# Splitting work moved between units of a gated two-branch Hedgehog linear-attention kernel, and three orders changed

## The chip, the cores and the metric

The kernel runs on one core of one Trainium2 chip. The time is the device time of one execution in microseconds (us), as the median of several runs; before the change it is 357.98 us (3 runs, 357.31 to 358.96). One of the five engines multiplies matrices (PE, with its weight loads shown apart as PEld); DVE, ACT and POOL work elementwise on tiles of 128 partitions; SP only issues DMAs. ACT issues some DMAs too. Each engine takes its instructions in the order in which the program gives them.

## The reference

```python
def _ref(x, wqkv, w_phi, wo):              # 16 heads of 28, x is 2048 x 448
    q, k, v = split((x @ wqkv))
    pq = einsum("bhsd,hdf->bhsf", q, w_phi)
    pk = einsum("bhsd,hdf->bhsf", k, w_phi)
    phi_q = concat([softmax(pq), softmax(-pq)])
    phi_k = concat([softmax(pk), softmax(-pk)])
    kv = einsum("bhsf,bhsd->bhfd", phi_k, v)
    z  = sum over s of phi_k
    o  = (phi_q @ kv) / (phi_q @ z + 1e-6)
    return o @ wo
g = sigmoid((x * gate_w).sum(-1))
out = g * _ref(x, A weights) + (1 - g) * _ref(x, B weights)
```

## The kernel before

The 2048 rows are 16 tiles of 128; two tiles make a unit, so each branch has 8 units, numbered here 0 to 7 for branch A and 8 to 15 for branch B. All matmuls on the inputs are done as three products of a high and a low part: `split_x` (L105) and `high_wv`/`low_wv`, `high_wo`/`low_wo` (L136, L139, L416, L420) make them. The high part is a copy on ACT (L108, L131), the low part a subtraction on POOL (L110, L112, L134) or DVE. `proj` (L172) makes one unit's queries, keys or values with 22 matmuls (11 for each tile, listed in `TERMS`, line L181) of 448 columns; x chunks 4 to 6 and the lower half of chunk 3 are low parts. The feature weights are folded into the key and query weights first: `fold` (L159) runs 32 small matmuls (L151) into two PSUM tiles, `fold_out` copies each on ACT (L156) and subtracts on DVE (L157).

A unit's keys go through `k_shift` (DVE L195 to L197, POOL L198), `k_exp` (two exponentials on ACT, L202), `k_sums` (two sums and a reciprocal on DVE, L211 and L212, then two normalising products on POOL, L220) and `kv_acc` (64 short matmuls on PE, L245), which adds the unit to the state. Queries go through `q_front` (L272, L274, and stores of `uq` to `qd` in DRAM, L281) and `q_load` (L289, `tq` back from DRAM), `q_exp0`, `q_min`, `q_exp1` (ACT L297, DVE L301, POOL L305, ACT L312) and `q_turn` (a DVE transposition into `wtb`, L315). `num` (L327) multiplies them with the state; `a_turn` (L524), `n_rec`, `n_den`, `weights` (L339 to L360) and `n_mul` (L365) turn, normalise and gate the numerators, `n_add` (L369) adds the halves. `wtb` (two buffers) also holds raw key and query weights, raw x and, from unit 2 on, the output weights that `load_wo` brings and `low_wo` sends back to DRAM (`wod`, L423 and L424) in two parts: part c lies in buffer (c // 2) % 2.

The order is that of the text. It is written in three stages: a prologue (L373 to L405) with unit 0's values; a loop over branch A's units (L431 to L502); a loop over branch B's units (L532 to L581), which also does branch A's numerators; and a last stage in which `STEPS` lists steps by hand, with the output products (L773), the copy of a finished tile `oc` (L783) and its store `sw` (L787). In branch A's loop two tables say in which unit the splits are made: `WVS` for branch B's value weights, `WOS` for the output weights. SP's queue takes loads and stores in program order, so a store that waits for data holds back all behind it. The PSUM work tiles called `two` are three, taken in turn.

Of the kernel before, what the change touches and what calls it, by code (L numbers as in the profile page):

```python
# [10 lines left out]
AF = mybir.ActivationFunctionType  # L11
# [3 lines left out]
P = 128  # L15
S, D, H, DH = 2048, 448, 16, 28
NT = S // P
# [32 lines left out]
def hedgehog_mix(ctx: ExitStack, tc: tile.TileContext, xd, wv, wkt, wqt, wphi, wo, cmask, cpmask, out):  # L50


    nc = tc.nc
# [40 lines left out]
    wvs = [wp_.tile([P, 2, 4, DG], F32R, name="wva"), wp_.tile([P, 2, 4, D], F32R, name="wvb")]  # L94
    wq = [wp_.tile([P, 2, 4, D], F32R, name="wqa"), None]
# [9 lines left out]
    def split_x(g, lo, hi, *parts):  # L105
        r, t, h = [a[:, :, lo * P:hi * P] for a in (xraw[g], xg[g], xg[g].bitcast(F32))]
        if 0 in parts:
            nc.scalar.activation(t[:, 0:4], r, AF.Copy)  # L108
        if 1 in parts:
            nc.gpsimd.tensor_tensor(t[64:P, 3], r[64:P, 3], h[64:P, 3], OP.subtract)  # L110
        if 2 in parts:
            nc.gpsimd.tensor_tensor(t[:, 4:7], r[:, 0:3], h[:, 0:3], OP.subtract)  # L112
# [31 lines left out]
    def two_tile(i=None):  # L144
        if i is None:
            i = turn[0] = (turn[0] + 1) % 3
        return twos[i].tile([P, 2, 512], F32, name=f"two{i}")
# [11 lines left out]
    def fold(b, wt, dst):  # L159
        for c in range(0, 4, 2):  # L160
            ps = two_tile()
            for g in range(4):
                fold_mm(b, wt, ps, g, c)
            fold_out(ps, dst, c)
# [7 lines left out]
    def proj(u, w, ps, order=None):  # L172
        n = w.shape[3]
        for i, j in order or [(i, j) for i in range(2) for j in range(11)]:
            if i is None:
                warm(j)
                continue
            t = 2 * u + i
            x, o = xg[t // 4], (t % 4) * P
            xc, k, wc = TERMS[j]  # L180
            nc.tensor.matmul(ps[:, i, :n], x[:, xc, o:o + P], w[:, k, wc], start=j == 0, stop=j == 10)  # L181
        return ps
# [7 lines left out]
    def k_shift(k, ps):  # L190
        p4 = hb(ps[:, :, :D])
        mx = ph.tile([P, 2, 2, H], F32, name="mx")
        e = es[k] = ph.tile([P, 2, HA * DH], F32, name="e")
        e5 = e.rearrange("p s (w h f) -> p s w h f", w=2, f=DH)
        nc.vector.tensor_reduce(mx[:, 0], p4, AX.X, OP.max)  # L195
        nc.vector.tensor_tensor(e5[:, 0], p4, mx[:, 0, :, :, None].to_broadcast([P, 2, H, DH]), OP.subtract)
        nc.vector.tensor_reduce(mx[:, 1], e5[:, 0], AX.X, OP.min)  # L197
        nc.gpsimd.tensor_tensor(e5[:, 1], mx[:, 1, :, :, None].to_broadcast([P, 2, H, DH]), e5[:, 0], OP.subtract)  # L198
# [23 lines left out]
    def k_sums(k):  # L222
        k_sums0(k)
        k_sums1(k)

    def v_out(k, ps):
        v = vs[k % 2]
        nc.scalar.activation(v[:, :, :, :, :DH].rearrange("p w j q f -> p w (j q) f"), hb(ps[:, :, :D]), AF.Copy)  # L228
        if k < NU:
            nc.scalar.activation(glog[:, 2 * k:2 * k + 2], ps[:, :, D], AF.Copy)  # L230
# [131 lines left out]
    def n_mul(k, lo=0, hi=8):  # L362
        c3 = cview(k).rearrange("p r s a m -> p (r s) a m")[:, :, lo:hi, :DH]
        dd = sms[k][1].rearrange("p r s a -> p (r s) a")[:, :, lo:hi, None]
        nc.gpsimd.tensor_tensor(c3, c3, dd.to_broadcast([P, 8, hi - lo, DH]), OP.mult)  # L365
# [22 lines left out]
    def warm(n):  # L388
        for i in range(n):
            nc.tensor.transpose(pw[:, 0, :P], ident, ident)  # L390
# [7 lines left out]
    for q in range(4):  # L398
        nc.vector.tensor_scalar(bd[:, :, :, q * DH:(q + 1) * DH], wp[:, :, :, :DH], mask[:, q:q + 1], None, op0=OP.mult)
    pv = proj(0, wvs[0], two_tile(), TERMS0)  # L400
    split_x(0, 2, 4, 0, 1, 2)
    v_out(0, pv)
    fold(0, wt, wk[0])
    split_x(1, 0, 4, 0, 1, 2)
    v_out(1, proj(1, wvs[0], two_tile()))  # L405


    def wo_part(c):
# [3 lines left out]
    def load_wo(*cs):  # L412
        for c in cs:
            nc.sync.dma_start(wo_part(c)[0], wos[:, HP * c:HP * (c + 1), :])
# [9 lines left out]
        nc.sync.dma_start(wod[1][:, c], st[0])  # L424


    WVS = {1: (0, 1, 2), 3: (3,)}
    WOS = {3: (0, 1), 5: (2, 3), 6: (4, 5), 7: (6,)}
    FRONTS = {2: 0, 5: 1}
    pq = None  # L430
    for u in range(NU):  # L431

        if u in (2, 4):
            split_x(u // 2 + 1, 0, 4, 0)
        for c in WVS.get(u, ()):
            high_wv(1, c)
        if u == 5:
            nc.gpsimd.memset(eq[:, :, :, :, DH:], 0.0)
            for b in range(2):
                nc.gpsimd.memset(kvs[b], 0.0)  # L440
        if pq is not None:
            q_front(FRONTS[u - 1], pq)
            q_load(FRONTS[u - 1])
            pq = None
        pk = proj(u, wk[0], two_tile())
        if u > 1:
            k_sums(u - 1)
        if u in (2, 4):
            split_x(u // 2 + 1, 0, 4, 1)
        k_shift(u, pk)  # L450
        if u == 1:
            k_sums(0)
        if u == 2:
            pq = proj(0, wq[0], two_tile())
            kv_acc(0)
        if u > 1:
            pv = proj(u, wvs[0], two_tile())
            v_out(u, pv)
        k_exp(u)

        if u == 0:
            wtqa = load_wt(wtb[0], wqt[0])
            load_x(2, 0, 4)
            for c in range(0, 4, 2):
                load_wv(1, c)
        if u == 1:
            wtkb = load_wt(wtb[1], wkt[1])
            nc.sync.dma_start(wos.rearrange("g (a f) n -> g a (f n)", f=DH),
                              wo.rearrange("(a g f) n -> g a (f n)", g=4, f=DH))
        if u in (2, 4):  # L470
            split_x(u // 2 + 1, 0, 4, 2)
        for c in WVS.get(u, ()):
            low_wv(1, c, nc.gpsimd)
        for c in WOS.get(u, ()):
            high_wo(c)
            low_wo(c)
        if u == 2:
            load_wo(0, 1)
            load_x(3, 0, 4)
        if u == 4:  # L480
            load_wo(2, 3)
        if u == 5:
            load_wo(4, 5)
            start.close()
            mid = ctx.enter_context(tc.tile_pool(name="mid", bufs=1, side="right"))
            wtqb = load_wt(mid.tile([P, 2048], F32, name="ctr"), wqt[1])
        if u == 6:
            load_wo(6)
        if u > 1:
            kv_acc(u - 1)  # L490
        if u == 1:
            fold(0, wtqa, wq[0])
        if u == 3:
            fold(1, wtkb, wk[1])
        if u == 5:
            pq = proj(FRONTS[u], wq[0], two_tile())
        if u == 6:
            q_exp0(0)
            q_min(0)
            q_exp1(0)  # L500
        if u == 7:
            q_turn(0)  # L502
# [29 lines left out]
    for u in range(NU):  # L532
        k = NU + u
        f, m, n = u + 2, u + 1, u - 1
        if u == 2:
            ctr[1] = mid.tile([P, 2048], F32, name="ctr")
        pq = proj(f % NU, wq[f // NU], two_tile())
        if n >= 0:
            a_turn(n)
            n_rec(n)  # L540
        q_exp0(m)
        q_min(m)
        q_exp1(m)
        if n >= 0:
            n_den(n)
            weights(n, nc.gpsimd)
            n_mul(n)
        else:
            k_sums(k - 1)
        q_front(f, pq)  # L550
        q_load(f)
        pk = proj(u, wk[1], two_tile())
        if u == 0:
            kv_acc(k - 1)
            state_copy(0)
        else:
            k_sums(k - 1)
        k_shift(k, pk)
        if u == 0:
            state_turn(0)  # L560
            q_turn(m)
            fold(1, wtqb, wq[1])
        pv = proj(u, wvs[1], two_tile())
        v_out(k, pv)
        k_exp(k)
        if u > 0:
            q_turn(m)
        if u == NU - 1:
            woh, wol = [wp_.tile([P, 7, D], F32R, name=n) for n in ("wkb", "wvb")]
            for w, d in ((woh, wod[0]), (wol, wod[1])):  # L570
                nc.sync.dma_start(w.bitcast(F32), d)
        if n >= 0:
            a_add(n)
        if u == 4:
            nc.gpsimd.tensor_scalar(gate[:, 1], gate[:, 0], -1.0, 1.0, op0=OP.mult, op1=OP.add)
        ts = nums[u] = [two_tile(), two_tile()]
        num(u, [t[:, i] for t in ts for i in range(2)])
        if u == 0:
            gates()
        else:  # L580
            kv_acc(k - 1)  # L581
# [4 lines left out]
    obs = [ob[:, i] for i in range(2)]  # L586
# [4 lines left out]
    nps, turns, outs = [], [None, None], [None, None]  # L591
# [188 lines left out]
        products(t, ((1, woh),))  # L780

    def oc(t):
        nc.scalar.activation(obs[t % 2], outs[t % 2][:, :D], AF.Copy)  # L783
        hls.pop(t)

    def sw(t):
        nc.sync.dma_start(out[t * P:(t + 1) * P, :], obs[t % 2])  # L787

    acts = dict(q=q, qf=qf, mx=mx, cp=cp, qs=qs, sq=sq, aq=aq, sl=sl, e0=e0, mn=mn, ms=ms, e1=e1, qt=qt, at=at, na=na, sa=sa, da=da,
                wa=wa, ma=ma, aa=aa, sd=sd, ks=ks, km=km, kv=kv, sc=sc, st=st, ss=ss, num=num_, bt=bt, nr=nr, sm=sm, nd=nd, wt=wt_,  # L790
# [47 lines left out]
```

## Time and profile before

| | before |
|---|---|
| median of 3 runs | 357.98 us (357.31 to 358.96) |
| profiled execution, its own time | 359.09 us |
| its span, first to last instruction | 357.2 us |
| granted TensorE clock, mean | 0.998 |
| DVE, ACT, POOL busy | 270.1, 121.8, 261.5 us |
| one load or store of a part of the output weights | 224 KB |
| load of `ctr`; one of the four stores of a unit's queries | 896 KB; 112 KB |

The profiled execution is 1.1 us above the median of the runs; 1.9 us of its time lie outside its span. PE is busy nearly the whole span, so the time can be read from the places where PE's next group of matmuls starts late. In a timeline row stand the start, the duration, the engine, the line, the operation with output and input tile, the count, and in brackets how long the engine had been idle and who ended that.

### The profile page before, as it was taken

Reading aid. Unit: us, or ns where it says so; the run is one execution under the profiler, and the core shown is the slowest. Engines: PE = TensorE matmul, PEld = TensorE weight load, DVE = VectorE, ACT = ScalarE, POOL = GpSimd, SP = SyncE. Lnnn points to the kernel's source line nnn. Section 1 sums busy time; section 2 is a strip of 40 time slices with the busy share of each in tenths; the row PEclk is TensorE's granted clock in tenths of the full one; section 3 lists DMA queues with packets and bytes.
Section 4 is the critical chain, followed back from the end, with each engine's and each line's share of the span. In section 5 each row is a group of like instructions: output and inputs, shape, how many; then the busy total and the mean of one; then the engine's idle time right before and its main releaser. Section 6 shows DMA issues by size and latency. Waiting matters only on the chain.

```text
span 357.2 us, 8435 instructions
## 1 busy us (share of the span) xinstructions
PE 346.2 (97%) x3599; PEld 304.6 (85%) x3599; DVE 270.1 (76%) x312; ACT 121.8 (34%) x171; POOL 261.5 (73%) x226
## 2 busy tenths in 40 slices
PE   7999899999999999999999999999999999999995
PEld 6889789988987889798898989888888978888894
DVE  4118765643967749998989898899899999988840
ACT  4433532534054241315133131412224454434331
POOL 2453897497476606988889788886779999999850
PEclk9999999999999999999999999999999999999999
DMA  7795225300753402241313332249662461664111
GB/s 236 221 319 173 114 79 193 135 25 14 210 157 141 129 1 61 75 126 61 103 54 104 106 104 65 94 162 352 160 226 84 140 196 57 180 180 128 53 52 51
DMA packets 33733, 45.75 MB, mean 128 GB/s; under 512 B 11408, under 2 KB 27008, under 8 KB 33408
## 3 DMA queue, kind: packets, MB, share of 16 engines
q1 hardware_dynamic: 28688, 41.20, 36.9%
q10 hardware_dynamic: 5008, 4.02, 3.5%
q8 instruction: 28, 0.46, 0.5%
q14 instruction: 9, 0.07, 0.1%
HBM read 27.29 MB, written 19.53 MB: 131 GB/s over the span
## 4 chain that ended last, share of the span: by engine, by line
PE 65%; DMA 12%; POOL 8%; DVE 8%; issue 3%; ACT 2%; SPq 1%; ACTq 0%; POOLq 0%; DVEq 0%
PE two L181 39%; PE out L773 16%; PE two L327 4%; DMA qd<-uq 4%; POOL e L220 3%; PE kv L245 3%; DMA xrb<-in_xt 2%; POOL xg L112 1%; DMA wtb<-wos 1%; DVE sm L211 1%; DVE wtb L315 1%; ACT e L202 1%; DMA wp<-in_wphi 1%; DMA wod<-wtb 1%; PE two L151 1%
## 5 line engine op out<-in xcount | busy, mean ns | idle before, releaser
L181 PE MATMUL two<-wka,xg 128*128 128x448 f32 x352 | 73.8, 365 | 0.0
L181 PEld LDWEIGHTS two<-wka,xg 128*128 128x128 f32 x352 | 65.2, 188 | 5.6 <-issue 0.8
L220 POOL TENSOR_TENSOR e<-e,rs 128x896 f32<-128x896 f32 x32 | 53.9, 1706 | 19.1 <-DVE rs L212 19.1
L228 ACT ACTIVATE vs<-two 128x896 f32<-128x896 f32 x16 | 14.7, 920 | 97.6 <-PE two L181 97.6
L181 PE MATMUL two<-wva,xg 128*128 128x450 f32 x176 | 39.4, 373 | 1.9 <-ACT wva L131 1.0
L211 DVE TENSOR_REDUCE sm<-e 128x32 f32<-128x896 f32 x32 | 33.1, 1077 | 8.6 <-ACT e L202 8.6
L181 PE MATMUL two<-wqa,xg 128*128 128x448 f32 x176 | 38.0, 371 | 1.0 <-DVE wqa L157 1.0
L315 DVE STREAM_TRANSPOSE wtb<-xrb 128x2048 f32<-128x2048 f32 x16 | 36.6, 2290 | 2.3 <-ACT glog L230 2.3
L181 PEld LDWEIGHTS two<-wva,xg 128*128 128x128 f32 x176 | 32.8, 189 | 6.2 <-POOL xg L112 1.1
L181 PE MATMUL two<-wvb,xg 128*128 128x448 f32 x176 | 37.2, 366 | 0.0
L181 PE MATMUL two<-wkb,xg 128*128 128x448 f32 x176 | 36.5, 362 | 0.0
L181 PEld LDWEIGHTS two<-wqa,xg 128*128 128x128 f32 x176 | 32.4, 188 | 4.8 <-DVE wqa L157 1.4
L198 POOL TENSOR_TENSOR e<-mx,e 128x896 f32<-128x896 f32 x16 | 27.3, 1704 | 12.5 <-DVE mx L197 9.2
L181 PEld LDWEIGHTS two<-wvb,xg 128*128 128x128 f32 x176 | 33.0, 188 | 2.7
L181 PEld LDWEIGHTS two<-wkb,xg 128*128 128x128 f32 x176 | 33.0, 188 | 2.3
L773 PE MATMUL out<-wkb,e 128*128 128x448 f32 x154 | 34.7, 369 | 0.1
L202 ACT ACTIVATE e<-e 128x896 f32<-128x896 f32 x32 | 28.7, 945 | 17.7 <-POOL e L198 17.6
L773 PEld LDWEIGHTS out<-wkb,e 128*128 128x128 f32 x154 | 28.5, 188 | 4.1 <-issue 0.8
L305 POOL TENSOR_TENSOR xrb<-qmn,tq 128x896 f32<-128x896 f32 x16 | 28.1, 1758 | 2.7 <-issue 2.2
L272 DVE TENSOR_REDUCE qmx<-two 128x32 f32<-128x896 f32 x14 | 15.1, 1077 | 16.6 <-PE two L181 16.6
L365 POOL TENSOR_TENSOR wva<-wva,cdd 128x896 f32<-128x896 f32 (+1 forms) x12 | 26.5, 2211 | 0.9
L365 POOL TENSOR_TENSOR ctr<-ctr,cdd 128x896 f32<-128x896 f32 (+1 forms) x12 | 26.5, 2209 | 0.6
(105 smaller groups left out, 583.5 us busy)
## 6 DMA issues: line engine op xcount, KB each, us to landing
tq<-qd SPq DMA_DIRECT2D x16, 448.0 KB, 4.7
qd<-uq ACTq DMA_DIRECT2D x32, 112.0 KB, 2.7
qd<-uq SPq DMA_DIRECT2D x32, 112.0 KB, 2.1
od<-wva SPq DMA_DIRECT2D x8, 448.0 KB, 2.5
wqa<-od SPq DMA_DIRECT2D x8, 448.0 KB, 4.4
out<-bd SPq DMA_DIRECT2D x16, 224.0 KB, 3.6
wod<-wtb SPq DMA_DIRECT2D x14, 224.0 KB, 2.0
xrb<-in_xt SPq DMA_DIRECT2D x2, 1024.0 KB
```

What stands on the lines that cost most here:

```text
L181: nc.tensor.matmul(ps[:, i, :n], x[:, xc, o:o + P], w[:, k, wc], start=j == 0, stop=j == 10)
L198: nc.gpsimd.tensor_tensor(e5[:, 1], mx[:, 1, :, :, None].to_broadcast([P, 2, H, DH]), e5[:, 0], OP.subtract)
L202: nc.scalar.activation(es[k][:, s], es[k][:, s], AF.Exp)
L211: nc.vector.tensor_reduce(sm[:, s], e[:, s].rearrange("p (h f) -> p h f", f=DH), AX.X, OP.add)
L220: nc.gpsimd.tensor_tensor(e3, e3, rs[:, s, :, None].to_broadcast([P, HA, DH]), OP.mult)
L228: nc.scalar.activation(v[:, :, :, :, :DH].rearrange("p w j q f -> p w (j q) f"), hb(ps[:, :, :D]), AF.Copy)
L272: nc.vector.tensor_reduce(mx, p4, AX.X, OP.max)
L305: nc.gpsimd.tensor_tensor(eq[:, 1, :, :, :DH], mn.rearrange("p c a -> p a c")[:, :, :, None].to_broadcast([P, 8, 4, DH]), tview(k), OP.sub ...
L315: nc.vector.transpose(wtb[k % 2], eq.rearrange("p s a c f -> p (s a c f)"))
L327: nc.tensor.matmul(banks[r][32 * g:32 * g + 32, 256 * s:256 * s + 256], kvt[b][32 * r:32 * r + 32, s, g], eT[32 * r:32 * r + 32, s, g], st ...
L365: nc.gpsimd.tensor_tensor(c3, c3, dd.to_broadcast([P, 8, hi - lo, DH]), OP.mult)
L773: nc.tensor.matmul(outs[t % 2][:, :D], (hi, lo)[x][:, c], w[:, c], start=x == 0 and n == 0 and c == 0, stop=x == 1 and c == 6)
```

## The change

The last two tiles of the first four x tiles are split one by one, not as a pair. Unit 1's values are projected with the terms in another order: for each tile first the six products that need only high parts of x (0, 1, 2, 7, 8, 9), then chunk 3 (6), then the low parts (3, 4, 5), then chunk 3 with the low weights (10). The splits of branch B's value weights go from units 1 and 3 to units 2 and 3. Those of output weights 4 and 5 go from unit 6 to unit 5 and part 6 from unit 7 to unit 6, with their loads a unit earlier. The query fold goes ahead of unit 0's key sums and unit 1's exponentials. In branch B's second unit the normalising products of unit 8's keys go ahead of unit 0's numerators. The last tile is copied out half by ACT and half by DVE, and stored by two DMAs.

```diff
-    split_x(0, 2, 4, 0, 1, 2)
+    for i in range(2, 4):
+        split_x(0, i, i + 1, 0, 1, 2)
...
-    v_out(1, proj(1, wvs[0], two_tile()))
+    v_out(1, proj(1, wvs[0], two_tile(), [(i, j) for i in range(2) for j in (0, 1, 2, 7, 8, 9, 6, 3, 4, 5, 10)]))
...
-    WVS = {1: (0, 1, 2), 3: (3,)}
-    WOS = {3: (0, 1), 5: (2, 3), 6: (4, 5), 7: (6,)}
+    WVS = {2: (0, 1), 3: (2, 3)}
+    WOS = {3: (0, 1), 5: (2, 3, 4, 5), 6: (6,)}
...
         if u == 1:
+            fold(0, wtqa, wq[0])
             k_sums(0)
...
         if u == 4:
-            load_wo(2, 3)
+            load_wo(2, 3, 4, 5)
         if u == 5:
-            load_wo(4, 5)
+            load_wo(6)
...
-        if u == 6:
-            load_wo(6)
         if u > 1:
             kv_acc(u - 1)
-        if u == 1:
-            fold(0, wtqa, wq[0])
...
             weights(n, nc.gpsimd)
-            n_mul(n)
+            if u > 1:
+                n_mul(n)
...
             k_sums(k - 1)
+            if u == 1:
+                n_mul(n)
...
     def oc(t):
-        nc.scalar.activation(obs[t % 2], outs[t % 2][:, :D], AF.Copy)
+        n = D if t < NT - 1 else D // 2
+        nc.scalar.activation(obs[t % 2][:, :n], outs[t % 2][:, :n], AF.Copy)
+        if n < D:
+            nc.vector.tensor_copy(obs[t % 2][:, n:], outs[t % 2][:, n:D])
...
     def sw(t):
-        nc.sync.dma_start(out[t * P:(t + 1) * P, :], obs[t % 2])
+        n = D if t < NT - 1 else D // 2
+        if n < D:
+            nc.scalar.dma_start(out[t * P:(t + 1) * P, :n], obs[t % 2][:, :n])
+        nc.sync.dma_start(out[t * P:(t + 1) * P, D - n:], obs[t % 2][:, D - n:])
```

On PE no group of matmuls changes its place. On DVE, in unit 1 of branch A, before (`wqa` is the folded query weight, `sm` and `rs` the sums and reciprocals of units 0 and 1, `two` the PSUM tile):

```order
L197 TENSOR_REDUCE mx<-e 128x32
L211 TENSOR_REDUCE sm<-e 128x32 x2
L212 RECIPROCAL rs<-sm 128x64
L157 TENSOR_TENSOR wqa<-two_378,wqa 128x896
L157 TENSOR_TENSOR wqa<-two_389,wqa 128x896
L211 TENSOR_REDUCE sm<-e 128x32 x2
L212 RECIPROCAL rs<-sm 128x64
```

And in the changed kernel, the same place on DVE:

```order
L197 TENSOR_REDUCE mx<-e 128x32
L157 TENSOR_TENSOR wqa<-two_364,wqa 128x896
L157 TENSOR_TENSOR wqa<-two_375,wqa 128x896
L211 TENSOR_REDUCE sm<-e 128x32 x2
L212 RECIPROCAL rs<-sm 128x64
L211 TENSOR_REDUCE sm<-e 128x32 x2
L212 RECIPROCAL rs<-sm 128x64
```

The two subtractions of the fold now stand ahead of unit 0's sums; on ACT the fold's two copies (L156) likewise stand ahead of unit 1's two exponentials, and the three copies of value weights that stood between are gone from there.

On SP, around units 4 to 6 of branch A, before (`wtb` holds output weights, `wos` is their rearranged copy in DRAM, `ctr` takes branch B's raw query weights, `qd` and `tq` are unit 1's queries on their way through DRAM):

```order
L414 DMA wtb_122<-wos 128x1x448 x2
L423 DMA wod_85<-wtb_122 128x448
L424 DMA wod_86<-wtb_122 128x448
L423 DMA wod_85<-wtb_122 128x448
L424 DMA wod_86<-wtb_122 128x448
L414 DMA wtb_121<-wos 128x1x448 x2
L117 DMA ctr<-in_wqt 112x4x512
L281 DMA qd_89<-uq_128 32x4x224 x2
L289 DMA tq_130<-qd_89 128x896
L423 DMA wod_85<-wtb_121 128x448
L424 DMA wod_86<-wtb_121 128x448
```

In the changed kernel, from the last of the loads of parts 4 and 5 on:

```order
L415 DMA wtb_121<-wos 128x1x448 x2
L424 DMA wod_85<-wtb_122 128x448
L425 DMA wod_86<-wtb_122 128x448
L424 DMA wod_85<-wtb_122 128x448
L425 DMA wod_86<-wtb_122 128x448
L424 DMA wod_85<-wtb_121 128x448
L425 DMA wod_86<-wtb_121 128x448
L424 DMA wod_85<-wtb_121 128x448
L425 DMA wod_86<-wtb_121 128x448
L415 DMA wtb_122<-wos 128x1x448
L117 DMA ctr<-in_wqt 112x4x512
L281 DMA qd_89<-uq_128 32x4x224 x2
```

Four more stores now stand ahead of the load of `ctr` and of unit 1's queries, which stood ahead of them.

On POOL, at the second unit of branch B, before (`cdd` are the weights of unit 0's numerators in `wva`, `e` the keys' features):

```order
L360 TENSOR_TENSOR cdd<-crs,cden 128x64
L365 TENSOR_TENSOR wva<-wva,cdd 128x64x28
L220 TENSOR_TENSOR e<-e,rs 128x896 x2
L198 TENSOR_TENSOR e<-mx,e 128x896
L369 TENSOR_TENSOR wva<-wva 128x4x8x28
```

And in the changed kernel:

```order
L360 TENSOR_TENSOR cdd<-crs,cden 128x64
L220 TENSOR_TENSOR e<-e,rs 128x896 x2
L365 TENSOR_TENSOR wva<-wva,cdd 128x64x28
L198 TENSOR_TENSOR e<-mx,e 128x896
L369 TENSOR_TENSOR wva<-wva 128x4x8x28
```

The long product on the numerators (L365) changes places with the two products on unit 8's keys (L220); the next units' order is as before.

## The prediction

> **What bounds the kernel now.** I read the page's busy line first, then the timeline of PE, then for each late start of PE the timelines of the engines it waited for.
>
> ```profile
> PE 346.2 (97%) x3599; PEld 304.6 (85%) x3599; DVE 270.1 (76%) x312; ACT 121.8 (34%) x171; POOL 261.5 (73%) x226
> ```
>
> PE is busy 346.2 of 357.2 us and the change takes no matmul away: what can be won are PE's late starts and the two ends. In PE's timeline I compare the distance between starts of neighbouring groups, since the modelled ends of matmuls overlap the next start.
>
> ```profile
> 16.56 0.86 PE L181 MATMUL two<-wva,xg 128*128 128x450 f32 x3
> 18.20 4.18 PE L181 MATMUL two<-wva,xg 128*128 128x450 f32 x19 [0.77 <-POOL xg L112]
> 22.22 8.98 PE L181 MATMUL two<-wka,xg 128*128 128x448 f32 x44
> ...
> 34.52 4.66 PE L181 MATMUL two<-wka,xg 128*128 128x448 f32 x22
> 40.16 4.75 PE L181 MATMUL two<-wqa,xg 128*128 128x448 f32 x22 [0.98 <-DVE wqa L157]
> ...
> 60.52 0.99 PE L245 MATMUL kv<-e,vs 128*29 128x56 f32 x64
> ...
> 94.22 4.68 PE L181 MATMUL two<-wva,xg 128*128 128x450 f32 x22
> 98.83 0.99 PE L245 MATMUL kv<-e,vs 128*29 128x56 f32 x64
> 99.76 4.67 PE L181 MATMUL two<-wka,xg 128*128 128x448 f32 x22
> 104.27 4.66 PE L181 MATMUL two<-wva,xg 128*128 128x450 f32 x22
> 109.79 0.99 PE L245 MATMUL kv<-e,vs 128*29 128x56 f32 x64 [0.86 <-POOL e L220]
> ...
> 115.31 4.57 PE L181 MATMUL two<-wkb,xg 128*128 128x448 f32 x22
> 120.34 0.99 PE L245 MATMUL kv<-e,vs 128*29 128x56 f32 x64 [0.46 <-POOL e L220]
> ...
> 144.48 1.50 PE L327 MATMUL two<-wtb,kvt 32*32 32x256 f32 x64
> 146.82 0.99 PE L245 MATMUL kv<-e,vs 128*29 128x56 f32 x64 [0.84 <-POOL e L220]
> ...
> 162.73 0.99 PE L245 MATMUL kv<-e,vs 128*29 128x56 f32 x64
> ```
>
> Undisturbed, 22 value matmuls take 98.83 - 94.22 = 4.61 us to the next start, 22 key or query matmuls 104.27 - 99.76 = 4.51. Against these, five starts are late: unit 1's values by (22.22 - 16.56) - 4.61 = 1.05; the first queries by (40.16 - 34.52) - 4.51 = 1.13; the state of unit 6 by (109.79 - 104.27) - 4.61 = 0.91; that of unit 7 by (120.34 - 115.31) - 4.51 = 0.52; that of unit 8, by its bracket, 0.84. Together **4.45 us**. Each of the five is where one part of the change works. Times below are those of the run of before; a shift says by how much PE has come forward by then.
>
> **The x tiles and the order of terms (1.05).**
>
> ```profile
> 14.33 1.06 ACT L108 ACTIVATE xg<-xrb 128x1024 fp32r<-128x1024 f32 x1 [4.48 <-DMA xrb<-in_xt]
> ...
> 9.98 0.46 POOL L110 TENSOR_TENSOR xg<-xrb,xg 64x128 fp32r<-64x128 f32 x1 [2.86 <-ACT xg L108]
> 10.52 1.01 POOL L112 TENSOR_TENSOR xg<-xrb,xg 128x384 fp32r<-128x384 f32 x1
> ...
> 17.09 2.09 DVE L157 TENSOR_TENSOR wka<-two,wka 128x896 fp32r<-128x896 f32 x2 [7.26 <-ACT wka L156]
> ```
>
> The copy of two tiles starts at 14.33, when the data lands; PE stopped after three matmuls, for the low part. Cut in two, each copy costs at least 0.53 and at most 1.06, so the first is done by 15.4; its subtractions for one tile take 9.98 to 11.53 = 1.55, to about 17.0 at the latest, the second tile's to 18.55. PE starts unit 1 at 16.56 and now has six products of 0.21 (4.61 / 22) that need no low part, until 17.82, and one more that needs L110 alone. The second tile is begun 11 x 0.21 = 2.3 later, at 18.87, after all of it is there. The wait goes wholly, even by the upper ends: **1.05**. The extra copy pushes ACT's next work back by at most 1.06, and with it the folded key weight, from 19.18 to 20.24 at worst; the keys now start at 22.22 - 1.05 = 21.17, so it costs nothing, with 0.9 to spare.
>
> **The fold ahead of exponentials and sums (1.13).**
>
> ```profile
> 31.98 1.79 ACT L202 ACTIVATE e<-e 128x896 f32<-128x896 f32 x2 [8.58 <-POOL e L198]
> ...
> 38.09 1.70 ACT L156 ACTIVATE wqa<-two 128x896 fp32r<-128x896 f32 x2
> ...
> 33.48 1.09 DVE L197 TENSOR_REDUCE mx<-e 128x32 f32<-128x896 f32 x1
> 34.49 2.07 DVE L211 TENSOR_REDUCE sm<-e 128x32 f32<-128x896 f32 x2
> 36.59 0.55 DVE L212 RECIPROCAL rs<-sm 128x64 f32<-128x64 f32 x1
> 39.02 2.09 DVE L157 TENSOR_TENSOR wqa<-two,wqa 128x896 fp32r<-128x896 f32 x2 [1.87 <-ACT wqa L156]
> ```
>
> The fold's matmuls end just before 34.52; ACT came to its copies only at 38.09, behind three copies of value weights and unit 1's exponentials. Now they follow unit 0's exponentials (done 33.77), and the second waits for PE: done at about 35.5. DVE, free at 34.57, subtracts until about 36.8, 2.2 us before the queries can start at 34.52 + 4.51 = 39.03. All **1.13** are won; with 1.05 the shift is 2.18. What is late next: unit 0's sums and reciprocal follow the subtractions (2.07 + 0.55, to 39.4), POOL's products on its keys take 3.37 (row at 95.01 below), to 42.9, and PE wants them at 39.03 + 4.51 = 43.5. Margin 0.6; if the fold's products ran a microsecond longer, 0.4 would come back here.
>
> **The splits of weights.** The three copies and subtractions of value weights leave unit 1; two go to unit 2, one more to unit 3.
>
> ```profile
> 55.33 3.37 POOL L220 TENSOR_TENSOR e<-e,rs 128x896 f32<-128x896 f32 x2 [1.39 <-DVE rs L212]
> ...
> 95.01 3.37 POOL L220 TENSOR_TENSOR e<-e,rs 128x896 f32<-128x896 f32 x2 [4.48 <-DVE rs L212]
> ...
> 102.41 2.28 POOL L134 TENSOR_TENSOR wtb<-wtb 128x448 fp32r<-128x448 f32 x2 [2.37 <-ACT wtb L131]
> ...
> 106.36 3.38 POOL L220 TENSOR_TENSOR e<-e,rs 128x896 f32<-128x896 f32 x2
> ...
> 110.11 2.31 DVE L315 STREAM_TRANSPOSE wtb<-xrb 128x2048 f32<-128x2048 f32 x1 [2.30 <-ACT glog L230]
> ...
> 105.77 4.21 DMA wod<-wtb
> ```
>
> A subtraction is 2.28 / 2 = 1.14. In unit 2 two of them meet 1.39 of idle POOL, 0.9 too little: the products at 55.33 end 0.9 later, at 59.6, before PE's state at 60.52. Cost nothing; uncovered, 0.9. In unit 5 the two added subtractions (2.28) meet 4.48 of idle at 95.01: nothing. In unit 6 one of two goes, so the products at 106.36 begin 1.14 sooner, end at 108.6, and PE can start at 104.27 + 4.61 = 108.88: **0.91** won, with a margin of 0.28 only. In unit 7 the profile names ACT for DVE's wait of 2.30 at 110.11, but that ACT work was long done; the chain of waits has the store of output weights from `wtb` there, landing at 109.98. Parts 4 and 5 are now stored a unit earlier, so the transposition, and behind it unit 7's sums, come up to 2.3 sooner, and POOL's last subtraction of unit 7 is gone: **0.52** won.
>
> **Products ahead of the numerators (0.84).**
>
> ```profile
> 140.99 0.55 DVE L212 RECIPROCAL rs<-sm 128x64 f32<-128x64 f32 x1
> ...
> 140.21 3.22 POOL L365 TENSOR_TENSOR wva<-wva,cdd 128x1792 f32<-128x1792 f32 x1
> ...
> 153.57 3.22 POOL L365 TENSOR_TENSOR ctr<-ctr,cdd 128x1792 f32<-128x1792 f32 x1
> 157.53 3.37 POOL L220 TENSOR_TENSOR e<-e,rs 128x896 f32<-128x896 f32 x2 [0.74 <-DVE rs L212]
> ```
>
> The keys' products now wait for their reciprocal, 141.54, rather than for L365: 141.6 to 145.0, ahead of PE's 145.98. **0.84** won. In exchange everything from L365 on slides: POOL's work from 140.21 to 153.57 has no gap, 13.36 us, and now starts at 141.6, so the next L365 starts at 155.0 instead of 153.57 and unit 9's products at 155.0 + 3.2 = 158.2 instead of 157.53, to 161.6. PE wants them at 162.73 - 0.84 = 161.89. Margin 0.3; without the 0.74 of idle the loss would be 0.7. After that unit POOL is back in step.
>
> **The last tile.**
>
> ```profile
> 352.99 0.54 ACT L783 ACTIVATE bd<-out 128x448 f32<-128x448 f32 x1 [3.72 <-PE out L773]
> 353.56 0.81 SPq L787 DMA_DIRECT2D out<-bd  x2
> ```
>
> Two stores end the kernel: tile 15's, and behind it on SP tile 14's, whole. Half a copy on ACT beside half on DVE costs between half of 0.54 and all of it, so both stores start 0 to 0.27 sooner; the halves add a DMA on ACT's queue beside SP's issue of 0.4 each. Bounds -0.3 to +0.4 (one issue), I take **0.2** won. The Trainium skill, DMA: Bandwidth & Descriptors, Anatomy of one DMA, speaks against small transfers: about 2.0 us fixed and bytes over 436 GB/s; by it a half of 115 KB lands an estimated 0.26 us before a whole, which would make the sum 0.26 larger if the half came last. No run here shows its fixed part by itself, and tile 14's whole store comes last.
>
> **The rivals.**
>
> *New waits take a third.* Three margins are 0.6 or less (units 0, 6 and 9). If each was missed by half a microsecond, 3.15 of the 4.65 below remain: 354.8. For it: POOL's spans are rough. Against it: each duration stands in a row.
>
> *Nothing comes through.* The last stage has a list of steps of its own; if DVE and POOL, not PE, set its pace, the time won ahead of it is waited off there: about 357.5, from the tail alone. Against it: PE's share is 97% over all.
>
> *The stores hold up the queries: slower.*
>
> ```profile
> 93.66 10.12 DMA qd<-uq
> ```
>
> Unit 1's queries go out on SP, behind the load of `ctr`, and landed 10.12 us after 93.66; only then are they read back. Four more stores of 224 KB now go ahead of them, one load of 224 KB less. In 93.66 to 103.78 some 1.8 MB were under way (two loads of 224 KB, `ctr` with 896, four quarters of 112 KB), 0.18 MB per us; 0.67 MB more at that rate is 3.8 us, plus 1 us for the later issue. At best the stores drain beside POOL's subtractions and it is 1 us. Read back by then, the queries meet DVE's L301 in front of unit 7's sums. PE wants unit 7's products at 120.34 - 0.91 - 0.52 = 118.9; less 3.37, 0.55, 2.07 and some 1.1 for L301, the queries must be back by about 111.7. Before they can have been back by 110 (DVE reads them soon after 110.11, unwaited): with 1 to 4.8 more, 111 to 114.8, so 0 to 3.1 us are lost there. It is slower than before only from 111.7 + 4.65 = 116.4 on, by over 0.5% from 118.2; at 120, 8.3 are lost and it takes 361.6. For it: one of these stores already took 10 us. Against: that needs another ten. The Trainium skill, same page, Queues, rings and completion order, says that each engine consumes descriptors in ring order; the trace's 10.12 behind `ctr` agrees, and by that rule alone the queries wait for the stores in full.
>
> **How the numbers follow.** The sum is 1.05 + 1.13 + 0.91 + 0.52 + 0.84 + 0.2 = 4.65. The profiled execution took 359.09, so 354.4 by it; it lay 1.1 above the median of 357.98, and against the median the forecast is 357.98 - 4.65 = **353.3**, chance 0.63 (352.2 to 354.4). New waits, 354.4 to 356.2: 0.22. Within 0.5% of before (1.8 us, about what a measurement of this kernel can tell from no change), 356.2 to 359.8: 0.08. Slower by the stores: 0.04. More than the sum, under 352.2: 0.03. So faster 0.88, same 0.08, slower 0.04. The range holds the forecast and new waits, and below it the tail's 0.3 and the medians' spread: 352.0 to 356.2.
>
> **What would show it.** In the profile after: no bracket at unit 1's values beyond the start, and 4.6 to the next group; the queries 4.5 after unit 2's keys; the three state groups with no idle ahead; DVE's transposition of unit 0's queries without its 2.3; the same distance as before from one unit's state to the next, from unit 9 on. Wrong it is if PE shows new idle at units 0, 7 or 9, if the first read of `tq` in branch B's loop waits for a DMA, or if the stretch from 265 on grew by what the start lost.

## The result and the profile after

The changed kernel takes 353.82 us (median of 4 runs, 353.64 to 354.23), the kernel before 357.64 us (4 runs): a ratio of 0.9899, 95% interval 0.9882 to 0.9915. That is 3.8 us less by the medians and 3.6 (3.0 to 4.2) by the ratio; forecast were 353.3 us and 4.65 less. The profiled execution took 353.85, its span is 352.1 us against 357.2. Of the 5.1 us between the two spans 0.86 lie ahead of unit 1's values (16.56 against 15.70 us), where the change does nothing; a second profile of the kernel before has 15.87 there.

The page's busy line of the changed kernel, and its timeline of PE at the five places of the prediction (late lines of the program have slightly higher numbers in the changed kernel):

```profile
PE 345.7 (98%) x3599; PEld 305.9 (87%) x3599; DVE 271.6 (77%) x313; ACT 121.7 (35%) x172; POOL 261.9 (74%) x228
...
15.70 4.77 PE L181 MATMUL two<-wva,xg 128*128 128x450 f32 x22
20.31 8.97 PE L181 MATMUL two<-wka,xg 128*128 128x448 f32 x44
...
32.60 4.66 PE L181 MATMUL two<-wka,xg 128*128 128x448 f32 x22
37.10 4.65 PE L181 MATMUL two<-wqa,xg 128*128 128x448 f32 x22
...
101.14 4.66 PE L181 MATMUL two<-wva,xg 128*128 128x450 f32 x22
105.73 0.99 PE L245 MATMUL kv<-e,vs 128*29 128x56 f32 x64
...
111.24 4.58 PE L181 MATMUL two<-wkb,xg 128*128 128x448 f32 x22
115.75 0.99 PE L245 MATMUL kv<-e,vs 128*29 128x56 f32 x64
...
139.91 1.50 PE L327 MATMUL two<-wtb,kvt 32*32 32x256 f32 x64
141.33 0.99 PE L245 MATMUL kv<-e,vs 128*29 128x56 f32 x64
...
157.22 0.99 PE L245 MATMUL kv<-e,vs 128*29 128x56 f32 x64
```

No row has a bracket. The five distances are 4.61, 4.50, 4.59, 4.51 and 1.42 us, as long as undisturbed groups: all five late starts are gone, and from 141.33 to 157.22 one unit takes 15.89, as before (146.82 to 162.73). From the state of unit 9 to PE's modelled end it is 190.18 us (157.22 to 347.40), before 190.17 (162.73 to 352.90): the last stage waits off nothing of what was won ahead of it. POOL's rows show how close PE's new times are to those of the products it takes (unit 0's are the first two of four):

```profile
37.63 6.69 POOL L220 TENSOR_TENSOR e<-e,rs 128x896 f32<-128x896 f32 x4 [3.20 <-DVE rs L212]
...
102.17 3.37 POOL L220 TENSOR_TENSOR e<-e,rs 128x896 f32<-128x896 f32 x2
...
153.65 3.37 POOL L220 TENSOR_TENSOR e<-e,rs 128x896 f32<-128x896 f32 x2
```

Unit 6's products end at 105.54 and PE takes them at 105.73; unit 9's end at 157.02, PE takes them at 157.22. Each has 0.2 us to spare; unit 0's, done at about 41.0, have 0.7 (PE's next start after the queries is 37.10 + 4.58 = 41.68).

The end is another matter. Timeline of the last microseconds, after PE's last matmul, whose modelled end is 347.40:

```profile
345.79 1.61 PE L774 MATMUL out<-wkb,e 128*128 128x448 f32 x7
...
347.48 0.36 ACT L785 ACTIVATE bd<-out 128x224 f32<-128x224 f32 x1 [3.72 <-PE out L774]
347.87 0.36 ACTq L793 DMA_DIRECT2D out<-bd  x1
347.87 0.39 DVE L787 COPY bd<-out 128x224 f32<-128x224 f32 x1 [6.54 <-ACT bd L785]
348.29 0.83 SPq L794 DMA_DIRECT2D out<-bd  x2
```

DVE's half starts at 347.87, when ACT's has ended (347.84), and DVE's bracket names ACT. The halves stand one behind the other, 0.78 us from the first start to the last end instead of 0.54. From PE's end to the end of the span it is 352.1 - 347.4 = 4.7 us, against 357.2 - (351.29 + 1.61) = 4.3 before.

### The profile page after: what moved, and what is told of

It reads as the page before. It is cut to its first block, busy times and chain, and to the rows that moved or that the text cites. A ratio compares the mean times of both kernels' runs of the same rounds, so it can differ in the third digit from the quotient of the medians.

```text
span 352.1 us, 8447 instructions
## 1 busy us (share of the span) xinstructions
PE 345.7 (98%) x3599; PEld 305.9 (87%) x3599; DVE 271.6 (77%) x313; ACT 121.7 (35%) x172; POOL 261.9 (74%) x228
## 4 chain that ended last, share of the span: by engine, by line
PE 81%; POOL 9%; DVE 5%; issue 1%; DMA 1%; ACT 1%; SPq 0%; POOLq 0%; ACTq 0%; DVEq 0%
PE two L181 50%; PE out L774 17%; PE two L327 5%; POOL e L220 3%; PE kv L245 3%; PE two L151 3%; POOL xg L112 2%; PE two L390 2%; DMA wtb<-wos 1%; DVE sm L211 1%; POOL e L198 1%; POOL wvb L134 1%; PE kv L327 1%; DVE wva L705 1%; POOL wtb L134 1%
## 5 line engine op out<-in xcount | busy, mean ns | idle before, releaser
L220 POOL TENSOR_TENSOR e<-e,rs 128x896 f32<-128x896 f32 x32 | 53.8, 1703 | 18.8 <-DVE rs L212 18.8
L305 POOL TENSOR_TENSOR xrb<-qmn,tq 128x896 f32<-128x896 f32 x16 | 28.2, 1760 | 3.5 <-issue 3.0
L365 POOL TENSOR_TENSOR wva<-wva,cdd 128x896 f32<-128x896 f32 (+1 forms) x12 | 26.5, 2210 | 0.8
L365 POOL TENSOR_TENSOR ctr<-ctr,cdd 128x896 f32<-128x896 f32 (+1 forms) x12 | 26.5, 2212 | 0.6
```

Of the source, the lines that this page charges most:

```text
L220: nc.gpsimd.tensor_tensor(e3, e3, rs[:, s, :, None].to_broadcast([P, HA, DH]), OP.mult)
L305: nc.gpsimd.tensor_tensor(eq[:, 1, :, :, :DH], mn.rearrange("p c a -> p a c")[:, :, :, None].to_broadcast([P, 8, 4, DH]), tview(k), OP.sub ...
```

## The experiments

Each run undoes one part in the changed kernel, unless told otherwise. The table has, for each kernel, the five distances of the prediction between starts on PE, the end (span less PE's modelled end, from the profile), the median, and the ratio to the kernel before on the same chip (its medians there were 357.29 to 357.64, so ratios compare better across rows than medians). Where the intervals of two ratios overlap, the times alone do not tell the kernels apart, and the argument rests on the distances. Distances that are not shown are as after, but for the rows of the kernel before and the last one.

| kernel | unit 1 values | first queries | state 6 | state 7 | state 8 | end | median us | ratio to before (95% interval) |
|---|---|---|---|---|---|---|---|---|
| before, first profile | 5.66 | 5.64 | 5.52 | 5.03 | 2.34 | 4.3 | 357.64 | |
| before, second profile | 5.24 | 5.64 | 5.51 | 4.74 | 2.60 | 4.3 | 357.57 | 1.0000 (0.9991 to 1.0010) |
| after | 4.61 | 4.50 | 4.59 | 4.51 | 1.42 | 4.7 | 353.82 | 0.9899 (0.9882 to 0.9915) |
| x tiles and terms undone | 5.17 | 4.49 | 4.60 | 4.50 | 1.43 | 4.2 | 354.39 | 0.9921 (0.9908 to 0.9935) |
| terms alone undone | 4.61 | 4.49 | 4.59 | 4.51 | 1.43 | 4.6 | 353.90 | 0.9897 (0.9882 to 0.9912) |
| x tiles alone undone | 4.61 | 4.50 | 4.58 | 4.51 | 1.43 | 4.2 | 354.04 | 0.9898 (0.9882 to 0.9913) |
| fold undone | 4.62 | 5.65 | 4.59 | 4.51 | 1.43 | 4.6 | 354.97 | 0.9936 (0.9923 to 0.9948) |
| output weights undone | 4.61 | 4.50 | 5.50 | 5.45 | 1.43 | 4.6 | 354.90 | 0.9930 (0.9916 to 0.9944) |
| part 6 alone in unit 7 | 4.61 | 4.49 | 4.59 | 4.51 | 1.43 | 4.7 | 354.09 | 0.9898 (0.9883 to 0.9914) |
| unit 0's numerators first | 4.60 | 4.50 | 4.59 | 4.51 | 1.82 | 4.7 | 354.48 | 0.9921 (0.9909 to 0.9933) |
| last tile whole | 4.62 | 4.50 | 4.85 | 4.50 | 1.42 | 4.5 | 353.71 | 0.9892 (0.9875 to 0.9910) |
| whole, tile 14 stored first | 4.61 | 4.50 | 4.59 | 4.50 | 1.42 | 3.9 | 353.21 | 0.9878 (0.9861 to 0.9896) |
| halves, tile 14 stored first | 4.61 | 4.50 | 4.60 | 4.51 | 1.43 | 3.9 | 353.12 | 0.9877 (0.9859 to 0.9894) |
| value weights in units 1, 3 | 4.61 | 4.49 | 4.59 | 4.51 | 1.42 | 4.7 | 356.21 | 0.9964 (0.9952 to 0.9977) |

**x tiles and terms.** Both undone:

```diff
-    for i in range(2, 4):
-        split_x(0, i, i + 1, 0, 1, 2)
+    split_x(0, 2, 4, 0, 1, 2)
...
-    v_out(1, proj(1, wvs[0], two_tile(), [(i, j) for i in range(2) for j in (0, 1, 2, 7, 8, 9, 6, 3, 4, 5, 10)]))
+    v_out(1, proj(1, wvs[0], two_tile()))
```

> The changed kernel with the last two x tiles split as a pair again and unit 1's values in the old order of terms. If the forecast's term holds, PE waits again three products into unit 1's values and the distance from their start to the next group grows from 4.61 to about 5.66 (1.05 us), with the median up by as much. Rival: the size of this wait hangs on when x lands (at 14.3 in the profile of before, at 13.0 in that after); then the distance grows by only 0.4 to 0.6 when x lands early, and the median with it. All later distances stay.

The distance grew to 5.17, by 0.56, and the median by 0.57 (by the ratios 0.8, within their intervals): the rival. The second profile of the kernel before says why.

> The kernel before once more, for a second profile. Theory: the profiled execution that the forecast was read from had x landing late (14.3) and PE's wait in unit 1's values too large; here x lands near 13, that distance is about 5.2 instead of 5.66, the span some 1 us shorter, and the sum of the five late starts 3.6 to 4.1 instead of 4.5. Rival: the same distances as in the first profile.

It is the theory: ACT's row of the copy of two x tiles, and PE's two rows in unit 1's values, in that second profile:

```profile
13.21 1.06 ACT L108 ACTIVATE xg<-xrb 128x1024 fp32r<-128x1024 f32 x1 [4.07 <-DMA xrb<-in_xt]
...
15.87 0.87 PE L181 MATMUL two<-wva,xg 128*128 128x450 f32 x3
17.09 4.18 PE L181 MATMUL two<-wva,xg 128*128 128x450 f32 x19 [0.35 <-POOL xg L112]
```

x was there at 13.21 instead of 14.33, while PE came 0.69 sooner (15.87 instead of 16.56), so the wait shrank from 0.77 to 0.35. The five late starts are 0.63 + 1.13 + 0.90 + 0.23 + 1.18 = 4.07 here; this execution took 357.98, near the median, the first one 359.09.

Each half alone:

> The changed kernel with the tiles split one by one but unit 1's terms in the old order. If the split alone does it, the first tile's low part is there for the fourth product and the distance stays at 4.6. If the order of terms is needed, it is 4.8 to 5.2.

> The changed kernel with the new order of terms but the two tiles split as a pair. The new order puts off the first need of a low part by three to four products (0.6 to 0.8 us), as much as the wait of 0.56 seen with both undone: the distance stays at 4.6. If the second chunk's need of the lower half comes too early, 4.7 to 5.0.

Either one suffices: the distance is 4.61 with the split alone and with the order alone. With x landing as late as in the first profile they may differ; that was not seen.

**The fold.**

```diff
         if u == 1:
-            fold(0, wtqa, wq[0])
             k_sums(0)
...
             kv_acc(u - 1)
+        if u == 1:
+            fold(0, wtqa, wq[0])
```

> The changed kernel with the query fold back at the end of unit 1, behind the sums of unit 0 and the exponentials of unit 1; the value weights' splits stay where the change put them. Forecast's theory: unit 1's exponentials alone hold the fold's copies back, so the queries start 5.6 instead of 4.5 after unit 2's keys, 1.1 us lost. Rival: the three copies of value weights were what held it back; then at most 0.3 is lost.

5.65, and 1.15 in the median: the exponentials alone hold the fold's copies back. ACT's rows there, without any value weights between:

```profile
34.27 1.80 ACT L202 ACTIVATE e<-e 128x896 f32<-128x896 f32 x2 [2.62 <-POOL e L198]
35.97 1.70 ACT L156 ACTIVATE wqa<-two 128x896 fp32r<-128x896 f32 x2
```

The exponentials wait 2.62 for POOL, and the copies, whose matmuls end before 32.40, wait with them.

**The value weights.** Only `WVS` is put back, with the fold left ahead:

```diff
-    WVS = {2: (0, 1), 3: (2, 3)}
+    WVS = {1: (0, 1, 2), 3: (3,)}
```

> The changed kernel with the splits of branch B's value weights back in units 1 and 3. They then stand ahead of the fold's copies on ACT and between unit 0's and unit 1's products on POOL. Theory of one move needing the other: the states of units 0 and 1 wait, together 1 to 1.9 us. Rival: they fit into idle time as before and nothing is lost.

Slower by 2.39. PE's distances to the states of units 0, 1, 2 and 4 are 5.21, 5.73, 4.89 and 5.19, where after has 4.58, 4.73, 4.59 and 4.78, in all 2.34 more. Units 0 and 1 lose 1.63 together, within what was expected; the 0.71 of units 2 and 4 were not expected. POOL and PE in that kernel:

```profile
38.82 3.36 POOL L220 TENSOR_TENSOR e<-e,rs 128x896 f32<-128x896 f32 x2 [4.46 <-DVE rs L212]
42.14 3.37 POOL L134 TENSOR_TENSOR wvb<-wvr,wvb 128x448 fp32r<-128x448 f32 x3
45.46 3.37 POOL L220 TENSOR_TENSOR e<-e,rs 128x896 f32<-128x896 f32 x2
...
42.23 0.99 PE L245 MATMUL kv<-e,vs 128*29 128x56 f32 x64 [0.56 <-POOL e L220]
...
48.88 0.99 PE L245 MATMUL kv<-e,vs 128*29 128x56 f32 x64 [0.94 <-POOL e L220]
```

The three subtractions stand between two units' products, and PE, no longer late for its own queries, waits for both. In the kernel before they cost nothing (4.69 and 4.72 to these two states, 4.67 and 4.73 in the run with the fold undone, where they are away), since the queries' wait covered them: the move of the table is a companion of the fold's, not a gain of its own. The state of unit 4, too, waits for POOL (its products end at 83.39, PE starts at 83.44); what made POOL late there was not followed up.

**The output weights.** All undone (`WOS` and the loads in units 4 to 6), and part 6 alone:

```diff
-    WOS = {3: (0, 1), 5: (2, 3, 4, 5), 6: (6,)}
+    WOS = {3: (0, 1), 5: (2, 3), 6: (4, 5), 7: (6,)}
...
-            load_wo(2, 3, 4, 5)
+            load_wo(2, 3)
```

```diff
-    WOS = {3: (0, 1), 5: (2, 3, 4, 5), 6: (6,)}
+    WOS = {3: (0, 1), 5: (2, 3, 4, 5), 7: (6,)}
```

> The changed kernel with the output weights' splits and loads back in units 5, 6 and 7. Forecast's theory: the states of units 6 and 7 wait again by 0.9 and 0.5, together 1.4 us. Rival: with the start 2.2 us earlier the waits have moved, and the move is worth under 0.5.

> The changed kernel with only part 6 of the output weights split in unit 7 again, its load where the change put it. If the store of parts 4 and 5 was what held DVE in unit 7, DVE's transposition still has no wait and unit 7's state starts within 0.3 of its place, since POOL had 1.3 of idle ahead of those products; the median rises by at most 0.3. If POOL's subtraction of part 6 was the cause, the state of unit 7 is late by 0.5 or more.

Undone, both states are late, by 0.91 and 0.94 in the profile and by 1.08 together in the median (that profiled execution, 355.65, was the slowest of five). The state of unit 7 thus varies: 0.52 and 0.23 late in the two profiles of before, 0.94 here. In the second profile of the kernel before, DVE's row of the transposition names its cause itself, and in the changed kernel the wait is gone:

```profile
109.47 2.31 DVE L315 STREAM_TRANSPOSE wtb<-xrb 128x2048 f32<-128x2048 f32 x1 [2.74 <-DMA wod<-wtb]
```

```profile
104.59 2.30 DVE L315 STREAM_TRANSPOSE wtb<-xrb 128x2048 f32<-128x2048 f32 x1
```

That wait is not the one that ended last ahead of unit 7's state, though. SP, ACT, DVE and POOL in the run with the output weights undone:

```profile
104.17 0.58 SPq L415 DMA_DIRECT2D wtb<-wos  x1
...
110.76 0.58 ACT L131 ACTIVATE wtb<-wtb 128x448 fp32r<-128x448 f32 x1 [0.61 <-DMA wtb<-wos]
...
112.86 0.55 DVE L212 RECIPROCAL rs<-sm 128x64 f32<-128x64 f32 x1
...
111.42 1.16 POOL L134 TENSOR_TENSOR wtb<-wtb 128x448 fp32r<-128x448 f32 x1 [3.10 <-ACT wtb L131]
112.54 1.77 POOL L305 TENSOR_TENSOR xrb<-qmn,tq 128x896 f32<-128x896 f32 x1
114.26 3.36 POOL L220 TENSOR_TENSOR e<-e,rs 128x896 f32<-128x896 f32 x2
```

Unit 7's sums and reciprocals are ready at 113.41, but POOL takes them only at 114.26: without a gap it first does part 6's subtraction (L134) and unit 1's queries (L305). That subtraction waits for ACT's copy, and the copy for the load of part 6, which SP issues behind the four stores of parts 4 and 5. In the two profiles of before and in this run the subtraction starts 1.23, 1.50 and 0.81 ahead of PE's group before the state (114.08, 112.71 and 111.42 against 115.31, 114.21 and 112.23), and the state is 0.52, 0.23 and 0.94 late: the two add up to 1.73 to 1.75 each time, while the reciprocals were ready 0.95, 0.21 and 0.85 before POOL took them. With part 6 alone back in unit 7, but its load still a unit earlier, the subtraction starts 2.14 ahead (109.34 against 111.48), state 7 stays at 4.51 and the median within 0.3. The subtraction thus costs nothing when its load is early; the late load with the subtraction behind it is what held unit 7. An estimate from the rows: with the transposition's wait alone, the products, 3.37 from the reciprocals on, would have been at most 0.1 late in any of the three.

**The numerators.**

```diff
             weights(n, nc.gpsimd)
-            if u > 1:
-                n_mul(n)
+            n_mul(n)
...
             k_sums(k - 1)
-            if u == 1:
-                n_mul(n)
```

> The changed kernel with unit 0's numerators normalised ahead of unit 8's products again. Forecast's theory: the state of unit 8 starts 2.3 instead of 1.4 after the numerators' matmuls, 0.9 us lost, and unit 9's keeps its distance. Rival: unit 8's products are in time anyway, since POOL now reaches them sooner; nothing lost.

State 8 was late by 0.40 in the profile and the median rose by 0.66; in the two profiles of before it was 0.92 and 1.18. What varies is the trip of the gate through DRAM, seen in POOL's row of the gate, first in the second profile of before, then in this run:

```profile
138.34 0.27 POOL L359 TENSOR_TENSOR cden<-cden,gate 128x32 f32<-128x32 f32 x1 [1.27 <-DMA gate<-gd]
```

```profile
134.61 0.28 POOL L359 TENSOR_TENSOR cden<-cden,gate 128x32 f32<-128x32 f32 x1 [0.49 <-DVE uq L274]
```

POOL's idle time there is 1.01, 1.27 and 0.49 in the first profile, the second and this run, and state 8 is 0.92, 1.18 and 0.40 late, 0.09 less each time. The bracket of the last one names DVE, but in all three the row starts 1.79 to 1.88 after SP has issued the gate's load (137.65, 136.46 and 132.82). When that load goes out early, POOL gets to its long product sooner and the old order costs less. The changed order takes that trip off the way to state 8.

**The last tile.** Whole copy and store again; then with tile 14's store ahead of tile 15's, whole and in halves:

```diff
-ol.15 oc.15 sw.15 sw.14
+ol.15 sw.14 oc.15 sw.15
```

> The changed kernel with the last tile copied whole by ACT and stored whole again. The profile after shows the DVE half starting only when the ACT half has ended, and 4.66 us from PE's last matmul to the end where before had 4.26. If the halves lengthen the end, this one is 0.4 us faster than the changed kernel and its end takes 4.3 again. Rival, the forecast's term: the halves save 0.2, and this one is 0.2 slower.

> As old_tail, and tile 14's store is issued ahead of tile 15's instead of behind it. Tile 14 is copied some 4 us before PE ends, so only one store of 224 KB is left at the end: if the queue's order sets the end, 0.6 to 1.0 us less than old_tail, an end of about 3.5. Rival: the end is the fixed time of the last store whatever goes beside it, and nothing changes.

> The changed kernel, last tile in halves, with tile 14's store ahead. If the two halves' copies stay one behind the other, the end is within 0.2 of tail_swap's; if halves do save once nothing is queued behind them, 0.3 us less than it.

The whole tile alone is 0.1 us faster than the halves by the medians, no more than the runs' spread; its end took 4.5 in the profile. Over the profiles with halves and the old queue the end ranges from 4.2 to 4.7, with the whole tile from 4.3 to 4.5: no saving by the halves is seen, and a loss of 0.1 to 0.3 cannot be told from none. In the profile with the whole tile, state 6 started 0.26 late, at 4.85: its margin of 0.2 does not hold in every execution. ACT's copy of part 6 waited there for its load, and POOL's subtraction and unit 6's products followed later, so the load that held unit 7 now stands ahead of unit 6:

```profile
98.94 0.58 ACT L131 ACTIVATE wtb<-wtb 128x448 fp32r<-128x448 f32 x1 [0.34 <-DMA wtb<-wos]
```

The queue's order does count: 0.5 us less with the whole tile (353.58 to 353.80 against 352.96 to 353.32, on one chip) and 0.7 less than after with halves, at 353.12 us the lowest median here (ratio to before 0.9877, 0.9859 to 0.9894). DVE's and SP's rows at the end, of the kernel with halves and tile 14 first:

```profile
347.75 0.39 DVE L787 COPY bd<-out 128x224 f32<-128x224 f32 x1 [6.54 <-ACT bd L785]
348.17 0.33 SPq L794 DMA_DIRECT2D out<-bd  x1
```

One issue of a half is left at the end where the changed kernel has two DMAs, the second of them a whole tile that had been ready since about 343.8. DVE waits for ACT here too.

## Why the prediction was right, and where it was off

- *All won lies in PE's late starts.* Right: all five are gone after, and each came back, in whole or in part, when its part was undone.
- *Unit 1's values, 1.05.* The mechanism was right, the term too large. It was read from an execution in which x landed at 14.33; in the other profiles it was between 12.5 and 13.3. It came back as 0.56 in the distance, 0.57 in the medians and 0.8 by the ratios, whose intervals overlap.
- *The fold, 1.13.* Right: 1.15 (1.3 by the ratios). That the value weights' copies counted for it was wrong; they only had to get out of POOL's way afterwards. What was written of unit 0's products, a margin of 0.6, came out as 0.7.
- *States 6 and 7, 0.91 and 0.52.* Unit 6 was right: 0.91 came back with POOL's second subtraction. For unit 7 the forecast followed the chain of waits through the store of parts 4 and 5 and DVE's transposition, and took POOL's last subtraction as a help. It was POOL that ended last, with the subtraction that stood behind part 6's late load. The change moves that load as well, so the gain came, in part by luck. Together 1.1 in the runs, state 7's share varying with the load's landing.
- *State 8, 0.84.* Right in cause; 0.66 in the runs (0.8 by the ratios, whose intervals overlap), varying with the gate's trip. Unit 9's products kept a margin of 0.2, forecast 0.3.
- *The last tile, 0.2.* Wrong, the one term that did not come at all: "Half a copy on ACT beside half on DVE costs between half of 0.54 and all of it". The two halves were never beside each other, and the copies took 0.78. The Trainium skill, PSUM — Partial Sum Buffer, PSUM bank collisions raise a hardware error, says that ACT and DVE must not access one bank in the same partitions at once, reads against reads included, and that the compiler back end's scheduler adds a dependency between such accesses; the row with DVE's start at 347.87 and the bracket on ACT agrees. The two halves also go into one SBUF tile, `bd`, which the bracket names. That this alone keeps two engines apart is unlikely, since in the changed kernel POOL begins to write into an `xg` tile at 13.75 while ACT's second copy into the same tile runs until 14.14:

```profile
12.99 1.15 ACT L108 ACTIVATE xg<-xrb 128x512 fp32r<-128x512 f32 x2 [4.28 <-DMA xrb<-in_xt]
...
13.75 0.45 POOL L110 TENSOR_TENSOR xg<-xrb,xg 64x128 fp32r<-64x128 f32 x1 [3.29 <-ACT xg L108]
```

That the halves stand one behind the other is shown; that the shared PSUM tile is the reason is argued, as no run puts them into two. The Trainium skill's fixed 2 us for a transfer (DMA: Bandwidth & Descriptors, Anatomy of one DMA), which that section gives for DMAs issued by GpSimd, is not shown by itself in any run here; these stores go out by SP and ACT.

- *The rivals.* No new wait took any of it in the profile after. The stores did not hold up the queries. On SP before, and then in the changed kernel, with DVE's first reading of them and PE's state of unit 5:

```profile
92.67 1.53 SPq L281 DMA_DIRECT2D qd<-uq  x2
103.90 0.34 SPq L289 DMA_DIRECT2D tq<-qd  x1
```

```profile
95.71 0.99 PE L245 MATMUL kv<-e,vs 128*29 128x56 f32 x64
...
92.28 0.93 SPq L281 DMA_DIRECT2D qd<-uq  x2
101.63 0.34 SPq L289 DMA_DIRECT2D tq<-qd  x1
...
106.82 1.04 DVE L301 TENSOR_REDUCE qmn<-tq 128x32 f32<-128x896 f32 x1
```

PE had come forward by 98.83 - 95.71 = 3.1 by then, so the read back was issued 0.9 later relative to PE, just under the 1 to 4.8 that were allowed, and DVE took it at 106.82 without a wait. From the end of the queries' issue to the read back it is 101.63 - 93.21 = 8.4 us, against 103.90 - 94.20 = 9.7 before: the four added stores did not lengthen it, and the queries did not wait for them in full.

By the medians the parts are worth 0.57 + 1.15 + 1.08 + 0.66 = 3.46, with 0.1 lost at the end 3.35, where 3.8 were measured; but these four were run on a chip on which the kernel before took 357.29. By the ratios, with 357.6 us as the whole, they are 0.8 + 1.3 + 1.1 + 0.8 = 4.0, with 0.25 lost 3.75, where 3.6 (3.0 to 4.2) were measured. Forecast were 4.65. The excess is x's 1.05 for 0.6 to 0.8, states 6 and 7 with 1.43 for 1.1, up to 0.2 of state 8, and the 0.2 of the last tile, which did not come. The forecast took the late starts from an execution of 359.09 and the time from the median of 357.98; the second profile, at 357.98, has 4.07 in place of 4.45.

## What to carry to other kernels

Where one engine is busy nearly throughout, compare the distances between its starts with undisturbed ones, and read each late start's cause from the rows of the engine it waited for; the two that engines alone set, the fold and unit 6, came back within 0.1 in the distances, and the three with a DMA's landing behind them were off by 0.4 to 0.5, so a second profile is worth having before those are sized. A wait that goes away need not be the one that ended last: compare when a result was ready with when it was taken. Here two engines that copied out of one PSUM tile did not work side by side. At the end of a kernel, look at what a queue still holds behind the last store: work that is ready should be issued ahead of it.

## What was not expected of the hardware

The same load of x, issued at 5.4 to 5.8, was there at 12.48 in one execution and at 14.33 in another, and with the old split and order the wait behind it ranged from 0.29 to 0.77 us; part 6's load moved state 7 between 0.23 and 0.94, the gate's trip state 8 between 0.40 and 1.18.
